# Decode attention: VectorE's eight unrolled heads become one loop whose semaphores are counted down

## The chip, the cores and the metric

One core of a Trainium2 chip. The metric is device time in microseconds (us) of one execution. A run is called fast when nothing marks it as slowed.

## The reference

```
B, Hq, Hkv, Sq, Sk, D = 1, 32, 8, 1, 65536, 128        # bf16 q, k, v
k = repeat(k, 4, axis=1); v = repeat(v, 4, axis=1)      # 4 query heads share one k/v head
scores = einsum("bhqd,bhkd->bhqk", q, k) * D ** -0.5
p = softmax(scores, axis=-1)
return einsum("bhqk,bhkd->bhqd", p, v)
```

k and v together are 268 MB and each byte is used once. Per k/v head there is one softmax over 65,536 keys for four query rows.

## The kernel before

`io` holds three slots of 64 KB per partition: slot 0 for half a head of v, slots 1 and 2 for the two halves (b = 0, 1) of a head of k. SyncE issues all loads on one DMA queue, in this order; each waits until PE has read what the slot held:

```
    load_k(0, 0); load_k(0, 1)
    for g in range(1, G):
        for b in range(2):
            load_k(g, b)          # waits for PE's scores of k(g-1, b):      s_sc
            load_v(g - 1, b)      # waits for PE's use of the v half before: s_vc
    load_v(G - 1, 0); load_v(G - 1, 1)
```

```
    def load_v(g, b):
        done = 2 * (2 * g + b)
        if (g, b) == (G - 1, 1):
            SP.wait((s_vc, done - 1))                     # first half of the last v
            load(v, g, b, 0, s_v[0], CUTS[0], CUTS[1])
            SP.wait((s_vc, done))
            ...                                           # the rest, in small pieces
        elif (g, b) in ((G - 2, 1), (G - 1, 0)):
            for i in range(2):                            # in two halves
                SP.wait((s_vc, done - 1 + i))
                load(v, g, b, 0, s_v[i], 128 * i, 128 * i + 128)
        else:
            SP.wait((s_vc, done))
            load(v, g, b, 0, s_v[0])
```

VectorE transposes k in place, finds the maximum, makes the bias, transposes the weights for PE (`weights`) and adds up the four partial sums of the output (`collect`). ACT does the exp and zeroes the PSUM accumulator (`clear`). PE already runs a loop. VectorE's program is unrolled by Python over the heads:

```
    for g in range(G):
        for _ in transposes(g, 0): pass
        for i, _ in enumerate(transposes(g, 1)):
            if i == 0 and g:
                DV.wait((s_vc, 4 * g - 2))
                weights(g - 1, 1)
        top(g)
        softmax(g)                       # issues ACT's exp too; for g == 0 also clear(0)
        if 0 < g < G - 1:
            weights(g, 0)
            DV.wait((s_vc, 4 * g))
            collected[g - 1] = collect()
            ACTQ.wait((s_dv, collected[g - 1]))
            clear(g)
        elif g:                          # the last head
            DV.wait((s_vc, 4 * g))
            DV.after(collect())
            collected[g - 1] = DV.mark(dve.memset(vacc, 0.0))
            weights(g, 0)
        else:                            # head 0: no collect
            weights(g, 0)
        if g: n_kept = keep(g - 1)
```

## Time and profile before

| | before |
|---|---|
| median of the first 3 runs | 630.67 us (630.35 to 631.05) |
| span of the profiled run | 628.4 us |
| bytes read | 268.44 MB, 427 GB/s over the span |
| VectorE busy | 54% |
| VectorE's program | 177 instructions |

From the page of the kernel before: the span, the DMA row (busy tenths in 40 slices of the span) and the list of DMA queues (kind: packets, MB, share of 16 engines).

```profile
span 628.4 us, 7102 instructions
...
DMA  8999999999999999999999999999999999999996
...
q1 hardware_dynamic: 6656, 268.45, 99.1%
q8 instruction: 1, 0.02, 0.0%
...
q14 instruction: 1, 0.01, 0.0%
```

The 16 DMA engines hardly ever rest (the packets of q1 fill 99.1% of their span), so the DMA queue is the bound here and everything else matters only if it leaves that queue, or one engine of it, without work. The page marks two packets as instruction; in the packet records they are 16,384 bytes at 624.0 us (queue 8) and 8,192 bytes at 221.2 us (queue 14). That such a packet is a part of a program being fetched is my reading; best_fetch below tests it for queue 14.

From the timeline of the kernel before (start us, duration us, engine, line, operation, tensors, count, and in brackets the idle time before it and what ended it): the end of head 0 with the v load that follows from it, a steady head, and the last head.

```profile
62.94 0.16 DVE L243 COPY nmb<-pb 128x1 f32<-128x1 f32 x1 [0.37 <-PE pb L462]
63.14 1.97 ACT L245 ACTIVATE ex<-acc,nmb 128x2048 bf16<-128x2048 f32 x1 [60.50 <-DVE nmb L243]
65.23 1.25 DVE L267 STREAM_TRANSPOSE et<-ex 128x1024 bf16<-128x1024 bf16 x1 [2.13 <-ACT ex L245]
65.29 2.31 ACT L256 ACTIVATE acc<-wz 128x2560 f32<-128x2560 bf16 x1
66.40 8.73 DVE L226 STREAM_TRANSPOSE io<-io 128x4096 uint32<-128x4096 uint32 x2
...
95.05 0.33 SPq L132 DMA_DIRECT2D io<-in_v_dram  x1
95.49 0.37 SPq L132 DMA_DIRECT2D io<-in_k_dram  x1
101.06 4.45 DVE L226 STREAM_TRANSPOSE io<-io 128x4096 uint32<-128x4096 uint32 x1 [17.29 <-DMA io<-in_k_dram]
...
372.73 17.30 DVE L226 STREAM_TRANSPOSE io<-io 128x8192 uint32<-128x8192 uint32 x2 [3.67 <-DMA io<-in_k_dram]
382.11 10.01 PE L420 MATMUL acc<-io,wz 128*128 x32 [9.65 <-PEq L114]
...
590.75 1.05 DVE L273 TENSOR_TENSOR vy<-acc,sely 128x512 f32<-128x512 f32 x1
590.87 1.97 ACT L245 ACTIVATE ex<-acc,nmb 128x2048 bf16<-128x2048 f32 x1 [63.27 <-DVE nmb L243]
591.83 0.69 DVE L279 TENSOR_REDUCE vs<-vy 128x128 f32<-128x512 f32 x1
592.70 0.48 DVE L313 MEMSET acc<- 128x512 f32 x1 [0.18 <-DVE vs L279]
593.37 0.59 PE L372 MATMUL pf<-vs,sel 128*4 128x130 f32 x2 [2.74 <-PEq L114]
595.66 3.59 PE L378 MATMUL acc<-io,et 128*16 128x512 bf16 x32 [1.70 <-PEq L114]
...
599.29 0.33 SPq L132 DMA_DIRECT2D io<-in_v_dram  x1
```

The second v of head 0 is issued at 95.05 us, and the k load ahead of it in the queue is seen by VectorE at 101.06: 6.0 us in hand. In a steady head VectorE waits 3.67 us for k. In the last head the first half of the last v is issued at 599.29 us.

### The profile page before, as it was taken

The numbers are of one execution on the slowest core, as the hardware profiler recorded it, in microseconds if no ns is written. First come the engines' busy times: TensorE is split into PE (matmuls) and PEld (weight loads), VectorE is DVE, ScalarE is ACT, GpSimd is POOL, SyncE is SP. The second block draws the span as 40 slices with busy tenths as digits, with TensorE's granted clock in tenths as the row PEclk, the third lists the DMA queues.
The fourth block names the chain that finished last, engine by engine and source line by source line (L and its number), as shares of the span: only waits on it lengthen the run. The fifth ranks groups of instructions, "written<-read, shape, count | busy, mean of one in ns | idle before, by whom it ended". The sixth has DMA issues, their size and how long they took to land. (4 is left out here: it accounts for less than half of the span.)

```text
span 628.4 us, 7102 instructions
## 1 busy us (share of the span) xinstructions
PE 349.1 (56%) x2126; PEld 137.0 (22%) x2126; DVE 339.2 (54%) x132; ACT 36.1 (6%) x32; POOL 7.5 (1%) x40
## 2 busy tenths in 40 slices
PE   0776482834837257372674816748066571876345
PEld 0222130311313023130221302213022230332112
DVE  3984835649065490654907548085570846684210
ACT  0000200020000200002000020000200002000100
POOL 1000000000000000000000000000000000000000
PEclk9999596976969769696696966959579695899666
DMA  8999999999999999999999999999999999999996
GB/s 368 434 467 401 405 463 405 463 413 455 421 446 413 455 405 463 401 467 401 467 401 467 401 467 401 463 405 463 405 463 405 463 405 463 401 436 434 434 434 271
DMA packets 6714, 268.48 MB, mean 427 GB/s; under 512 B 824, under 2 KB 1080, under 8 KB 1464
## 3 DMA queue, kind: packets, MB, share of 16 engines
q1 hardware_dynamic: 6656, 268.45, 99.1%
q8 instruction: 1, 0.02, 0.0%
q10 hardware_dynamic: 56, 0.01, 0.0%
q14 instruction: 1, 0.01, 0.0%
HBM read 268.44 MB, written 0.01 MB: 427 GB/s over the span
## 5 line engine op out<-in xcount | busy, mean ns | idle before, releaser
L420 PE MATMUL acc<-io,wz 128*128 x1024 | 269.2, 414 | 183.8 <-PEq L114 180.1
L226 DVE STREAM_TRANSPOSE io<-io 128x4096 uint32<-128x4096 uint32 (+1 forms) x54 | 279.0, 5207 | 164.9 <-DMA io<-in_k_dram 164.9
L420 PEld LDWEIGHTS acc<-io,wz 128*128 x1024 | 105.4, 103 | 347.8 <-issue 268.0
L378 PE MATMUL acc<-io,et 128*16 128x512 bf16 x1016 | 69.0, 416 | 22.1 <-PEq L114 21.5
L231 DVE TENSOR_REDUCE mg<-acc 128x1 f32<-128x2048 f32 x8 | 18.3, 2292 | 52.8 <-PE acc L420 52.8
L245 ACT ACTIVATE ex<-acc,nmb 128x2048 bf16<-128x2048 f32 x8 | 15.7, 1967 | 531.5 <-DVE nmb L243 531.5
L372 PE MATMUL pf<-vs,sel 128*4 128x130 f32 (+1 forms) x20 | 5.7, 386 | 62.6 <-PEq L114 62.6
L378 PEld LDWEIGHTS acc<-io,et 128*16 128x16 bf16 x1016 | 26.3, 94 | 61.4 <-issue 38.2
L267 DVE STREAM_TRANSPOSE et<-ex 128x1024 bf16<-128x1024 bf16 x16 | 19.6, 1224 | 29.7 <-ACT ex L245 14.9
L256 ACT ACTIVATE acc<-wz 128x2560 f32<-128x2560 bf16 x7 | 16.1, 2307 | 17.9 <-DVE vs L279 17.8
L372 PEld LDWEIGHTS pf<-vs,sel 128*4 128x4 f32 x20 | 1.2, 83 | 63.0 <-issue 63.0
L273 DVE TENSOR_TENSOR vy<-acc,sely 128x512 f32<-128x512 f32 x8 | 7.8, 980 | 11.9 <-PE acc L378 11.9
L235 DVE TENSOR_REDUCE m<-pt 1x4 f32<-1x128 f32 x8 | 2.2, 279 | 21.1 <-PE pt L460 21.1
L358 POOL COPY wz<-qT 32x16 bf16<-32x16 bf16 x32 | 6.1, 191 | 518.0 <-PE acc L420 435.5
L445 PE MATMUL pt<-et 128*16 128x512 bf16 x16 | 6.6, 410 | 0.0
L279 DVE TENSOR_REDUCE vs<-vy 128x128 f32<-128x512 f32 x7 | 4.8, 686 | 0.2
L462 PE MATMUL pb<-ident,nrow 1*128 1x1 f32 x8 | 1.5, 189 | 5.7 <-PEq L114 5.7
L460 PE MATMUL pt<-ident,mg 128*1 128x128 f32 x8 | 2.2, 270 | 2.5 <-PEq L114 2.5
L189 DVE MEMSET acc<- 128x2560 f32 x1 | 2.2, 2192 | 1.6 <-SPq L62 1.6
L243 DVE COPY nmb<-pb 128x1 f32<-128x1 f32 x8 | 1.3, 158 | 3.0 <-PE pb L462 3.0
L462 PEld LDWEIGHTS pb<-ident,nrow 1*128 1x128 f32 x8 | 1.1, 133 | 7.0 <-issue 7.0
L292 ACT ACTIVATE fall<-pf 4x130 f32<-4x130 f32 x7 | 1.9, 269 | 7.7 <-PE pf L372 7.7
(28 smaller groups left out, 17.8 us busy)
## 6 DMA issues: line engine op xcount, KB each, us to landing
io<-in_v_dram SPq DMA_DIRECT2D x5, 4096.0 KB, 16.8
io<-in_k_dram SPq DMA_DIRECT2D x4, 4096.0 KB, 25.9
io<-in_k_dram SPq DMA_DIRECT2D x4, 2048.0 KB, 40.3
io<-in_v_dram SPq DMA_DIRECT2D x1, 2048.0 KB, 10.8
io<-in_v_dram SPq DMA_DIRECT2D x1, 1024.0 KB, 12.9
io<-in_v_dram SPq DMA_DIRECT2D x3, 256.0 KB, 13.3
io<-in_v_dram SPq DMA_DIRECT2D x2, 128.0 KB, 13.3
io<-in_k_dram SPq DMA_DIRECT2D x13, 44.2
```

The source lines that it names most:

```text
L226: dve.transpose(out=part, in_=part).then_inc(s_kt, n // 32)
L231: dve.tensor_reduce(out=mg[:, :], in_=sc, axis=AX.X, op=ALU.max).then_inc(s_mg, 1)
L245: n = ACTQ.mark(act.activation(out=ex[:, :, :].rearrange("p b n -> p (b n)"), in_=sc, func=ACT.Exp, bias=nmb[:, :], scale=SCALE, accum_out ...
L256: cleared[g] = ACTQ.mark(act.activation(out=acc[:, :], in_=wz[:, 0, 0:1].to_broadcast([P, 5 * 512]), func=ACT.Copy))
L267: dve.transpose(out=et[:, :, :].rearrange("p i n -> p (i n)"), in_=ex[:, 2 * b:2 * b + 2, :].rearrange("p i n -> p (i n)"),).then_inc(s_et, 1)
L273: n = DV.mark(dve.tensor_tensor(out=vy[:, :, :].rearrange("p d y -> p y d") if not last else vz, in0=vacc, in1=sely[:, :, None].to_broadca ...
L279: return DV.mark(dve.tensor_reduce(out=vs[:, 0:D], in_=vy[:, :, :], axis=AX.X, op=ALU.add))
L358: gp.tensor_copy(out=wz[r, :, c0:c0 + H].rearrange("p (s w) h -> p s w h", s=2), in_=qTb[r, :, :, g, :],).then_inc(s_w, 1)
L372: return pe.matmul(out=pf[0:H, 0:w], lhsT=sel[:, :], rhs=vs[:, 0:w], skip_group_check=True, **kw)
L378: return pe.matmul(out=vacc[32 * c:32 * c + 16, :, :], lhsT=et[:, ch // 2, w0:w0 + 16], rhs=io[:, PS * ch + 4 * tt:PS * ch + 4 * tt + 4, : ...
L420: i = pe.matmul(out=bass.AP(acc, r_o, [[2560, P], [1, 512]]), lhsT=bass.AP(wz, r_w + ((2 * s + e) * WB - 4 * u), [[4 * WB, P], [1, P]]), r ...
L445: pe.matmul(out=pt[0:16, :], lhsT=et[:, 0, 0:16], rhs=et[:, 0, :], start=True, stop=True)
```

## The change

VectorE's program becomes one loop over the heads, 75 instructions in all, for 177. The loop's code has the same numbers to wait for in every pass, so each semaphore is taken down again after its wait, by an instruction of its own (the trace of the changed kernel has 116 EVENT_SEMAPHORE records on VectorE, the kernel before 25). What VectorE waits for must then be signalled once per head to VectorE alone: SyncE passes on "v half used" (`s_vd`), GpSimd "scores done" (`s_sd`).

```
-    for g in range(G):
-        ...                                    # the unrolled heads, as above
+    with nc.body("dve_head", valid_engines=only_d):
+        nc.regs_alu(r_g, r_g, 1, op=ALU.add)
+        transposes(0, 0, SL)                   # always pieces of 64, four per half
+        transposes(1, 0, 128)
+        d_take(s_vd)
+        weights(1)                             # in head 0 too, on zeros
+        transposes(1, 128, SL)
+        d_take(s_sd)
+        ...                                    # maximum, bias: d_take before each step
+        d_take(s_ex)
+        weights(0)
+        d_take(s_vd)
+        dve.tensor_tensor(out=vy..., in0=vacc, in1=sely..., op=ALU.mult).then_inc(s_ds, 1)
+        d_take(s_ds)
+        dve.tensor_reduce(out=vs[:, 0:D], in_=vy..., op=ALU.add).then_inc(s_dv, 1)
+        nc.br_cmp(r_g, G, "dve_head", "dve_tail", "IS_LT", engines=only_d)

+    for g in range(G):                         # ACT stays unrolled
+        ACTQ.wait((s_dv, d_nmb(g)))
+        act.activation(out=ex..., in_=sc, func=ACT.Exp, ...).then_inc(s_ex, 1)
+        ...
+        ACTQ.wait((s_dv, collected(g - 1)))
+        n_clear[g] = ACTQ.mark(act.activation(out=acc[:, :], in_=wz..., func=ACT.Copy))

     def load_v(g, b):
-            SP.wait((s_vc, done))
+            values_done(done)                  # the same wait, then sem_inc(s_vd, 1)
```

(Cut: the semaphores' counts given ahead, GpSimd's relay, a GpSimd memset of `ex`, PE's semaphore names.) Three things besides the loop move with it, since every pass must be alike: head 0 gets a `weights(1)` and a collect, and its clear now follows the collect; in the last head collect comes after `weights(0)`, not under the exp; and an ACT clear of 2560 columns takes the place of VectorE's 0.48 us memset.

More of the change, by code (lines that the diff above doesn't have):

```diff
@@ L12 @@
 PE = mybir.EngineType.PE
+DVE = mybir.EngineType.DVE
+POOL = mybir.EngineType.Pool
 P = 128
@@ L109 @@
     s_sc, s_pe, s_vb, s_vc = sem("s_sc"), sem("s_pe"), sem("s_vb"), sem("s_vc")
+    s_sd, s_vd, s_pt, s_ex, s_ds = sem("s_sd"), sem("s_vd"), sem("s_pt"), sem("s_ex"), sem("s_ds")
     def down(eng, which, s, n, wait=False):
@@ L134, in load, with values_done @@
         ).then_inc(s, 16)
-    k_cuts = {(0, 0): [0, 128, 256], (0, 1): [0, 128, 256], (G - 1, 1): [0, 64, 128, 192, 256]}
-    s_k = {(b, lo): sem(f"s_k{b}_{lo}") for b, lo in ((0, 0), (0, 128), (1, 0), (1, 64), (1, 128), (1, 192))}
-    k_count = {}
-    k_ready = {}
+    k_lo = {0: [0, 128], 1: [0, 64, 128, 192]}
+    s_k = {(b, lo): sem(f"s_k{b}_{lo}") for b in k_lo for lo in k_lo[b]}
     def load_k(g, b):
         SP.wait((s_sc, 16 * g - 8 + 8 * b if g else 0))
-        cuts = k_cuts.get((g, b), [0, SL])
+        if g == 1:
+            sp.sem_inc(s_k[b, 128], 16 * (G - 1 - b))
+        cuts = [0, 128, SL] if g == 0 else [0, 64, 128, 192, SL] if (g, b) == (G - 1, 1) else [0, SL]
         for lo, hi in zip(cuts, cuts[1:]):
-            k_ready[g, b, lo] = key = s_k[b, lo], k_count.get((b, lo), 0) + 16
-            k_count[b, lo] = key[1]
-            load(k, g, b, 1 + b, key[0], lo, hi)
+            load(k, g, b, 1 + b, s_k[b, lo], lo, hi)
+    def values_done(n):
+        SP.wait((s_vc, n))
+        if n:
+            sp.sem_inc(s_vd, 1)
     def load_v(g, b):
@@ L158, in load_v @@
         elif (g, b) in ((G - 2, 1), (G - 1, 0)):
-            for i in range(2):
-                SP.wait((s_vc, done - 1 + i))
-                load(v, g, b, 0, s_v[i], 128 * i, 128 * i + 128)
+            SP.wait((s_vc, done - 1))
+            load(v, g, b, 0, s_v[0], 0, 128)
+            values_done(done)
+            load(v, g, b, 0, s_v[1], 128, SL)
         else:
-            SP.wait((s_vc, done))
+            values_done(done)
             load(v, g, b, 0, s_v[0])
-            sp.sem_inc(s_v[1], 16)
     load_k(0, 0)
     load_k(0, 1)
-    sp.sem_inc(s_v[2], 16)
     for g in range(1, G):
@@ L182 @@
     GP.mark(gp.memset(vs[:, :], 0.0))
+    GP.mark(gp.memset(ex[:, :, :], 0.0))
     n = GP.mark(gp.memset(ident[:, :], 0.0))
@@ L188 @@
     ))
-    n = DV.mark(dve.memset(acc[:, :], 0.0))
-    collected = {-2: n, -1: n}
+    gp.sem_inc(s_vd, 2)
+    for s, n in ((s_k[1, 64], 16 * (G - 1)), (s_k[1, 192], 16 * (G - 1)), (s_v[1], 16 * (2 * G - 3)), (s_v[2], 16)):
+        gp.sem_inc(s, n)
+    DV.mark(dve.memset(acc[:, :], 0.0))
     DV.wait((s_gp, p_ident))
@@ L208, with d_nmb, collected @@
         ))
+    def d_nmb(g):
+        return d_qT + 2 * g + 1
+    def collected(g):
+        return d_qT + 2 * g + 4
+    d_last = collected(G - 2) + 6
     qTb = qT[:, :, :].rearrange("p s n -> p (s n)").bitcast(bf16).rearrange(
@@ L213 @@
     )
-    def transposes(g, b):
-        for t0 in range(0, SL, 128):
-            if (g, b, t0) in k_ready:
-                DV.wait(k_ready[g, b, t0])
-            n = 128 if 1 < g < G - 1 and b == 0 else 64
-            for t in range(t0, t0 + 128, n):
-                if t > t0 and (g, b, t) in k_ready:
-                    DV.wait(k_ready[g, b, t])
-                part = io[:, (1 + b) * SL + t:(1 + b) * SL + t + n, :]
-                part = part.rearrange("p t d -> p (t d)").bitcast(u32)
-                dve.transpose(out=part, in_=part).then_inc(s_kt, n // 32)
-            yield
@@ L229, in top @@
-    def top(g):
-        DV.wait((s_sc, 16 * g + 16))
-        dve.tensor_reduce(out=mg[:, :], in_=sc, axis=AX.X, op=ALU.max).then_inc(s_mg, 1)
-    def softmax(g):
-        DV.wait((s_pe, 3 * g + 2))
-        n = DV.mark(dve.tensor_reduce(
-            out=m4[:, :], in_=pt[0:1, 0:P].rearrange("o (x h) -> o h x", h=H), axis=AX.X, op=ALU.max
-        ))
-        DV.after(n)
-        dve.tensor_scalar_mul(
-            out=nrow[:, :, :], in0=m4[:, None, :].to_broadcast([1, 32, H]), scalar1=-SCALE
-        ).then_inc(s_nr, 1)
-        DV.wait((s_pe, 3 * g + 3))
-        d_nmb = DV.mark(dve.tensor_copy(out=nmb[:, :], in_=pb[:, 0:1]))
-        ACTQ.wait((s_dv, d_nmb))
-        n = ACTQ.mark(act.activation(
-            out=ex[:, :, :].rearrange("p b n -> p (b n)"), in_=sc, func=ACT.Exp,
-            bias=nmb[:, :], scale=SCALE, accum_out=vs[:, D + g % 2:D + g % 2 + 1],
-        ))
-        exped[g] = n
-        if g == 0:
-            ACTQ.wait((s_gp, p_ident))
-            ACTQ.after(n)
-            clear(0)
@@ L255, in clear @@
-    def clear(g):
-        cleared[g] = ACTQ.mark(act.activation(
-            out=acc[:, :], in_=wz[:, 0, 0:1].to_broadcast([P, 5 * 512]), func=ACT.Copy
-        ))
-    exped = {}
-    cleared = {}
-    def weights(g, b):
-        if b == 0:
-            DV.wait((s_ac, exped[g]))
-        dve.transpose(
-            out=et[:, :, :].rearrange("p i n -> p (i n)"),
-            in_=ex[:, 2 * b:2 * b + 2, :].rearrange("p i n -> p (i n)"),
-        ).then_inc(s_et, 1)
-    def collect(last=False):
-        n = DV.mark(dve.tensor_tensor(
-            out=vy[:, :, :].rearrange("p d y -> p y d") if not last else vz, in0=vacc,
-            in1=sely[:, :, None].to_broadcast([P, 4, D]), op=ALU.mult,
-        ))
-        DV.after(n)
-        if not last:
-            return DV.mark(dve.tensor_reduce(
-                out=vs[:, 0:D], in_=vy[:, :, :], axis=AX.X, op=ALU.add
-            ))
-        n = DV.mark(dve.tensor_tensor(
-            out=vz[:, 0:2, :], in0=vz[:, 0:2, :], in1=vz[:, 2:4, :], op=ALU.add
-        ))
-        DV.after(n)
-        return DV.mark(dve.tensor_tensor(
-            out=vs[:, 0:D], in0=vz[:, 0, :], in1=vz[:, 1, :], op=ALU.add
-        ))
@@ L290, in keep @@
-    def keep(g):
-        ACTQ.wait((s_pe, 3 * g + 7))
-        return ACTQ.mark(act.activation(out=fall[:, g, :], in_=pf[0:H, 0:D + 2], func=ACT.Copy))
-    for g in range(G):
-        for _ in transposes(g, 0):
-            pass
-        for i, _ in enumerate(transposes(g, 1)):
-            if i == 0 and g:
-                DV.wait((s_vc, 4 * g - 2))
-                weights(g - 1, 1)
-        top(g)
-        softmax(g)
-        if 0 < g < G - 1:
-            weights(g, 0)
-            DV.wait((s_vc, 4 * g))
-            collected[g - 1] = collect()
-            ACTQ.wait((s_dv, collected[g - 1]))
-            clear(g)
-        elif g:
-            DV.wait((s_vc, 4 * g))
-            DV.after(collect())
-            collected[g - 1] = DV.mark(dve.memset(vacc, 0.0))
-            weights(g, 0)
-        else:
-            weights(g, 0)
-        if g:
-            n_kept = keep(g - 1)
@@ L319 @@
-    DV.wait((s_ac, n_kept), (s_vc, 4 * G - 2))
-    weights(G - 1, 1)
-    o7 = io[0:H, SL:SL + G - 1, :]
-    for i in range(2):
-        n = DV.mark(dve.reciprocal(out=r7[:, i::2], in_=fall[:, i::2, D + i]))
-    DV.after(n)
-    n = DV.mark(dve.tensor_tensor(
-        out=o7, in0=fall[:, :, 0:D], in1=r7[:, :, None].to_broadcast([H, G - 1, D]),
-        op=ALU.mult,
-    ))
-    SP.wait((s_dv, n))
-    sp.dma_start(
-        out=out[0, 0:(G - 1) * H, 0, :].rearrange("(g h) d -> h g d", h=H), in_=o7
-    ).then_inc(s_st, 16)
@@ L334 @@
-    DV.wait((s_vb, 2 * G))
-    collected[G - 1] = collect(True)
-    DV.wait((s_pe, 3 * G + 2))
-    d_rl = DV.mark(dve.reciprocal(out=rl[:, :], in_=pl))
-    ACTQ.wait((s_dv, d_rl), (s_pe, 3 * G + 3))
-    n = ACTQ.mark(act.activation(out=o[:, :], in_=fin, func=ACT.Copy, scale=rl[:, :]))
-    ACTQ.after(n)
-    act.dma_start(out=out[0, (G - 1) * H:G * H, 0, :], in_=o[:, :]).then_inc(s_st, 16)
-    ACTQ.wait((s_st, 32))
-    for g in range(G):
-        if g == 0:
-            GP.wait((s_dv, d_qT))
-            GP.after(p_ident)
-        else:
-            GP.wait((s_sc, 16 * g))
-        for a in range(4):
-            r = slice(32 * a, 32 * a + 32)
-            c0 = 28 + 32 * a
-            if a == 3:
-                GP.wait(
-                    (s_dv, collected[g - 2]), (s_ac, cleared.get(g - 1, 0))
-                )
-            gp.tensor_copy(
-                out=wz[r, :, c0:c0 + H].rearrange("p (s w) h -> p s w h", s=2),
-                in_=qTb[r, :, :, g, :],
-            ).then_inc(s_w, 1)
@@ L362, with take @@
-    GP.wait((s_sc, 16 * G), (s_dv, collected[G - 2]), (s_ac, exped[G - 1]))
-    gp.sem_inc(s_w, 4)
-    def take(s, n):
-        down(pe, PE, s, n, wait=True)
+    def take(eng, which, s, n=1):
+        down(eng, which, s, n, wait=True)
     IO = 3 * SL * D
@@ L398 @@
     with block("pe_head"):
-        take(s_w, 4)
+        take(pe, PE, s_w, 4)
         gather(D + 2, start=True, stop=True).then_inc(s_pe, 1)
@@ L415 @@
         r_o = o8 * 16
-        take(s_kt, 1)
+        take(pe, PE, s_kt, 1)
         for u in range(2):
@@ L433 @@
     with block("pe_values"):
-        take(s_et, 1)
+        take(pe, PE, s_et, 1)
         for ch in range(4):
@@ L438 @@
             elif ch != 1:
-                take(s_v[ch // 2], 16)
+                take(pe, PE, s_v[ch // 2], 16)
             for tt in range(16 if ch < 3 else (SL - TAIL) % PS // 4):
@@ L458 @@
     with block("pe_softmax"):
-        take(s_mg, 1)
-        pe.transpose(out=pt[0:1, 0:P], in_=mg[:, :], identity=ident[:, :]).then_inc(s_pe, 1)
-        take(s_nr, 1)
+        take(pe, PE, s_mg, 1)
+        pe.transpose(out=pt[0:1, 0:P], in_=mg[:, :], identity=ident[:, :]).then_inc(s_pt, 1)
+        take(pe, PE, s_nr, 1)
         pe.transpose(
             out=pb[:, 0:1], in_=nrow[:, :, :].rearrange("o x h -> o (x h)"), identity=ident[0:1, 0:1]
-        ).then_inc(s_pe, 1)
+        ).then_inc(s_pt, 1)
         nc.br("pe_head", engines=only)
@@ L468 @@
         out=pl, lhsT=sel[:, :], rhs=vs[:, D + (G - 1) % 2:D + (G - 1) % 2 + 1], start=True, stop=True
-    ).then_inc(s_pe, 1)
+    ).then_inc(s_pt, 1)
     for t in range(SL - TAIL, SL):
@@ L474 @@
         if t == CUTS[-2]:
-            pe.wait_ge(s_dv, collected[G - 1])
+            pe.wait_ge(s_dv, d_last)
             gather(D, start=False, stop=False)
@@ L482, with d_take, transposes, weights @@
     i.then_inc(s_pe, 1)
+    def d_take(s, n=1):
+        take(dve, DVE, s, n)
+    def transposes(b, lo, hi):
+        for t in range(lo, hi, 64):
+            if t in k_lo[b]:
+                d_take(s_k[b, t], 16)
+            part = io[:, (1 + b) * SL + t:(1 + b) * SL + t + 64, :].rearrange("p t d -> p (t d)").bitcast(u32)
+            dve.transpose(out=part, in_=part).then_inc(s_kt, 2)
+    def weights(b):
+        dve.transpose(
+            out=et[:, :, :].rearrange("p i n -> p (i n)"),
+            in_=ex[:, 2 * b:2 * b + 2, :].rearrange("p i n -> p (i n)"),
+        ).then_inc(s_et, 1)
@@ new lines @@
+    only_d = OrderedEngineSet([DVE])
+    r_g = nc.alloc_registers("g", engines=only_d)
+    nc.regs_mov(r_g, 0)
+    nc.br("dve_head", engines=only_d)
+    with nc.body("dve_head", valid_engines=only_d):
[6 more added lines that the diff above has]
+        d_take(s_sd)
+        dve.tensor_reduce(out=mg[:, :], in_=sc, axis=AX.X, op=ALU.max).then_inc(s_mg, 1)
+        d_take(s_pt)
+        dve.tensor_reduce(
+            out=m4[:, :], in_=pt[0:1, 0:P].rearrange("o (x h) -> o h x", h=H), axis=AX.X, op=ALU.max
+        ).then_inc(s_ds, 1)
+        d_take(s_ds)
+        dve.tensor_scalar_mul(
+            out=nrow[:, :, :], in0=m4[:, None, :].to_broadcast([1, 32, H]), scalar1=-SCALE
+        ).then_inc(s_nr, 1)
+        d_take(s_pt)
+        dve.tensor_copy(out=nmb[:, :], in_=pb[:, 0:1]).then_inc(s_dv, 1)
+        d_take(s_ex)
+        weights(0)
+        d_take(s_vd)
+        dve.tensor_tensor(
+            out=vy[:, :, :].rearrange("p d y -> p y d"), in0=vacc,
+            in1=sely[:, :, None].to_broadcast([P, 4, D]), op=ALU.mult,
+        ).then_inc(s_ds, 1)
+        d_take(s_ds)
+        dve.tensor_reduce(out=vs[:, 0:D], in_=vy[:, :, :], axis=AX.X, op=ALU.add).then_inc(s_dv, 1)
+        nc.br_cmp(r_g, G, "dve_head", "dve_tail", "IS_LT", engines=only_d)
@@ new lines @@
+    nc.switch_bb("dve_tail")
+    DV.n = collected(G - 2)
+    n_clear, n_kept = {}, 0
+    for g in range(G):
+        ACTQ.wait((s_dv, d_nmb(g)))
+        act.activation(
+            out=ex[:, :, :].rearrange("p b n -> p (b n)"), in_=sc, func=ACT.Exp,
+            bias=nmb[:, :], scale=SCALE, accum_out=vs[:, D + g % 2:D + g % 2 + 1],
+        ).then_inc(s_ex, 1)
+        if g == 0:
+            ACTQ.wait((s_gp, p_ident))
+        ACTQ.wait((s_dv, collected(g - 1)))
+        n_clear[g] = ACTQ.mark(act.activation(
+            out=acc[:, :], in_=wz[:, 0, 0:1].to_broadcast([P, 5 * 512]), func=ACT.Copy
+        ))
+        if g:
+            ACTQ.wait((s_pe, g + 2))
+            n_kept = ACTQ.mark(act.activation(
+                out=fall[:, g - 1, :], in_=pf[0:H, 0:D + 2], func=ACT.Copy
+            ))
@@ new lines @@
+    DV.wait((s_ac, n_kept), (s_vd, 1))
+    weights(1)
+    o7 = io[0:H, SL:SL + G - 1, :]
+    for i in range(2):
+        n = DV.mark(dve.reciprocal(out=r7[:, i::2], in_=fall[:, i::2, D + i]))
+    DV.after(n)
+    n = DV.mark(dve.tensor_tensor(
+        out=o7, in0=fall[:, :, 0:D], in1=r7[:, :, None].to_broadcast([H, G - 1, D]),
+        op=ALU.mult,
+    ))
+    SP.wait((s_dv, n))
+    sp.dma_start(
+        out=out[0, 0:(G - 1) * H, 0, :].rearrange("(g h) d -> h g d", h=H), in_=o7
+    ).then_inc(s_st, 16)
@@ new lines @@
+    DV.wait((s_vb, 2 * G))
+    n = DV.mark(dve.tensor_tensor(
+        out=vz, in0=vacc, in1=sely[:, :, None].to_broadcast([P, 4, D]), op=ALU.mult
+    ))
+    DV.after(n)
+    n = DV.mark(dve.tensor_tensor(
+        out=vz[:, 0:2, :], in0=vz[:, 0:2, :], in1=vz[:, 2:4, :], op=ALU.add
+    ))
+    DV.after(n)
+    n = DV.mark(dve.tensor_tensor(
+        out=vs[:, 0:D], in0=vz[:, 0, :], in1=vz[:, 1, :], op=ALU.add
+    ))
+    assert n == d_last
+    DV.wait((s_pt, 1))
+    d_rl = DV.mark(dve.reciprocal(out=rl[:, :], in_=pl))
@@ new lines @@
+    ACTQ.wait((s_dv, d_rl), (s_pe, G + 2))
+    n = ACTQ.mark(act.activation(out=o[:, :], in_=fin, func=ACT.Copy, scale=rl[:, :]))
+    ACTQ.after(n)
+    act.dma_start(out=out[0, (G - 1) * H:G * H, 0, :], in_=o[:, :]).then_inc(s_st, 16)
+    ACTQ.wait((s_st, 32))
+    for g in range(G):
+        if g == 0:
+            GP.wait((s_dv, d_qT))
+            GP.after(p_ident)
+        else:
+            GP.wait((s_sc, 16 * g))
+            gp.sem_inc(s_sd, 1)
+        for a in range(4):
+            r = slice(32 * a, 32 * a + 32)
+            c0 = 28 + 32 * a
+            if a == 3 and g == 1:
+                take(gp, POOL, s_et)
+            if a == 3 and g:
+                GP.wait((s_ac, n_clear[g - 1]))
+            gp.tensor_copy(
+                out=wz[r, :, c0:c0 + H].rearrange("p (s w) h -> p s w h", s=2),
+                in_=qTb[r, :, :, g, :],
+            ).then_inc(s_w, 1)
@@ L486 @@
+    GP.wait((s_sc, 16 * G))
+    gp.sem_inc(s_sd, 1)
+    GP.wait((s_ac, n_clear[G - 1]))
+    gp.sem_inc(s_w, 4)
 _INS = ['q', 'k', 'v']
```

## The prediction

> What bounds the kernel now. The DMA engines. The page shows them 90% busy or more in every slice but the first and the last, 268.45 MB in a span of 628.4 us. The chain of waits ends in the last loads of v (landing at 622.3 us) and about 3.5 us of PE and ACT. At a head's end VectorE still waits 3.66 us for the next k (timeline, 369.08 to 372.73), and a v load is issued 5.7 to 9.9 us before the loads queued ahead of it have landed. So small delays on VectorE are covered.
>
> What the change removes. [...]the page lists one instruction packet of 0.01 MB on queue 14, and the packet records place it about 221 us into the span. The 64 KB data packet beside it took 3.08 us, its neighbours 2.42 us. From then on one of the 16 DMA engines is 0.75 us behind, for good, since no engine idles: its last data packet ends 0.8 us after the next engine's. [...]this lag sits on the final chain. [...]I take the fetch to be VectorE's; it goes away. Worth 0.7 us.
>
> What it adds.
> - Countdown waits: instructions of their own, [...] Covered by the 3.66 us.
> - Transposes of k(b=0) in four pieces, not two (17.42 us against 17.30): PE starts some 4 us earlier in five heads; no gain, since DMA bounds.
> - Head 0: one more weights transpose (1.2 us) and collect (1.7 us), so the first matmuls of head 1 come 1.7 us later and the v load issued at 95.05 us moves to 96.8; the queue has work until 101. GpSimd's memset of ex (about 2 us) falls into the 7.75 us that VectorE waits for the first k. Covered.
> - The branch back: [...]no refetch.
> - Last head: before, collect overlapped the exp, and a 0.48 us VectorE memset cleared; the gather ran at 593.37 us. Now weights(0), collect, a 2.31 us ACT clear and a relay follow each other: gather at about 598.8, v matmuls (3.59 us) at 599.5 instead of 595.66. The first half of the last v is issued at about 603.1 instead of 599.28, while the half before it lands at about 604.6. An issue takes about 1.5 us to first data (start of the run), so the DMA may idle 0 to 0.5 us here, the one place where the longer chain can show; I charge 0.2 us.
>
> Sum: 630.67 - 0.7 + 0.2 = about 630.1 us; 629.4 to 630.9 in 8 of 10. Faster by over 2%: 0.01; within 2%: 0.98; slower by over 2%: 0.01.
>
> What would show it. The DMA list has no instruction packet on queue 14 within the span; no single DMA engine lags at the end; the v landing in the final chain comes some 0.5 us earlier; the last head's gather is near 598.8 us and the v issue after it near 603; each head's first k reaches PE about 4 us sooner.
>
> What would make it wrong: the branch back stalls VectorE by over 4 us per head, the v issue in the last head falls over 1.5 us behind, or the page fetched at 221 us is not VectorE's.

What the trace of the kernel before shows: the packet on queue 14 has 8,192 bytes and begins at 221.2 us; in the loads' landing times, the last of 16 is 0.22 us behind the median at 197.7 us and 0.96 us at 237.2; and PE's wait for v on `s_v[2]`, in the final chain, ends at 622.38 us, after the last of the 16 landings of that load (622.34) and not after the median one (621.37). That the packet is VectorE's and worth 0.7 us was an estimate from that lag, 0.75 us in the packet records. The memset of `ex`, "about 2 us", took 1.81 us in the changed kernel's trace.

## The result

Six runs of each: 631.77 us median (630.22 to 632.80) against 630.65 (630.28 to 631.36). The ratio is 1.0017, 95% interval 1.0002 to 1.0031: within 2% as forecast, but outside the range, and on the other side of the kernel before. A ratio here is the mean time of one kernel's fast runs over that of the other's of the same rounds, so it isn't quite the ratio of the medians.

The page of the changed kernel, the same rows:

```profile
span 630.3 us, 7233 instructions
...
DMA  8999999999999999999999999999999999999986
...
q1 hardware_dynamic: 6656, 268.45, 98.8%
q8 instruction: 1, 0.02, 0.0%
```

The packet on queue 14 is gone, as predicted. But the DMA row has an 8 in its second last slice, where the kernel before has a 9: something ran dry near the end.

The timeline of the changed kernel, the same places:

```profile
63.56 0.16 DVE L394 COPY nmb<-pb 128x1 f32<-128x1 f32 x1 [0.49 <-DVEq L118]
65.96 1.25 DVE L366 STREAM_TRANSPOSE et<-ex 128x1024 bf16<-128x1024 bf16 x1 [2.24 <-DVEq L118]
67.13 1.02 DVE L399 TENSOR_TENSOR vy<-acc,sely 128x512 f32<-128x512 f32 x1
68.29 0.69 DVE L404 TENSOR_REDUCE vs<-vy 128x128 f32<-128x512 f32 x1
68.90 8.76 DVE L363 STREAM_TRANSPOSE io<-io 128x4096 uint32<-128x4096 uint32 x2
69.08 2.31 ACT L421 ACTIVATE acc<-wz 128x2560 f32<-128x2560 bf16 x1 [3.26 <-DVE vs L404]
...
97.65 0.33 SPq L136 DMA_DIRECT2D io<-in_v_dram  x1
98.03 0.42 SPq L136 DMA_DIRECT2D io<-in_k_dram  x1
100.37 4.45 DVE L363 STREAM_TRANSPOSE io<-io 128x4096 uint32<-128x4096 uint32 x1 [14.06 <-DVEq L118]
...
372.94 17.43 DVE L363 STREAM_TRANSPOSE io<-io 128x4096 uint32<-128x4096 uint32 x4 [3.10 <-DVEq L118]
378.06 7.34 PE L290 MATMUL acc<-io,wz 128*128 x24 [4.88 <-PEq L118]
...
593.64 1.25 DVE L366 STREAM_TRANSPOSE et<-ex 128x1024 bf16<-128x1024 bf16 x1 [2.24 <-DVEq L118]
594.81 1.01 DVE L399 TENSOR_TENSOR vy<-acc,sely 128x512 f32<-128x512 f32 x1
595.97 0.69 DVE L404 TENSOR_REDUCE vs<-vy 128x128 f32<-128x512 f32 x1
596.69 2.31 ACT L421 ACTIVATE acc<-wz 128x2560 f32<-128x2560 bf16 x1 [3.20 <-DVE vs L404]
599.19 0.59 PE L242 MATMUL pf<-vs,sel 128*4 128x130 f32 x2 [8.10 <-PEq L118]
600.03 3.59 PE L248 MATMUL acc<-io,et 128*16 128x512 bf16 x32 [0.26 <-PEq L118]
...
603.66 0.33 SPq L136 DMA_DIRECT2D io<-in_v_dram  x1
```

Three readings. The steady head is as forecast: VectorE still waits 3.10 us for k, and PE starts 4 us sooner (378.06 for 382.11). In head 0 the transposes start 2.50 us later (68.90 for 66.40): 0.73 us of it was there when `weights(0)` began (65.96 for 65.23), from the slower waits (in the rows, 0.49 for 0.37 us and 2.24 for 2.13) and a 0.28 us later start of the head's end; the rest is the collect. So the v load comes at 97.65 us, 2.6 us later, with 2.7 us in hand and not 6.0. In the last head that v half comes at 603.66 us, 4.4 us later.

**What one DMA engine did.** The busy rows average 16 engines. The trace also has every data packet with start, duration and size, without its engine; but the data packets fill 99.1% of the 16 engines' span (98.8% in the changed kernel), so they can be strung together, each to the chain that had just ended. That gives 16 chains and, where a chain pauses, an idle time. The lists below are worked out that way; their clock starts about 11 us before the span. Before, one chain pauses for 0.31 us for the instruction packet, then has a slow packet (3.08 us for 64 KB, its neighbours 2.42). In the changed kernel:

```
one chain    idle 1.11 us at 110.7, its next packet 3.23 us (others 2.42)     second v of head 0
15 chains    idle 0.8 to 2.9 us at 614 to 617, then 1.5 to 2.0 us for 32 KB (others 1.21)   last v
```

The load of 97.65 us finds one of 16 engines already idle. The chain with that pause is 1.72 us behind the median chain when the last head begins, has no pause over 0.3 us in the dry stretch, and still ends last of all: 1.0 us after the median chain. It isn't untouched there, though: its own landings come 1.4 us late after the dry stretch (see "What the landings show").

### The profile page after: what moved, and what is told of

Read it like the earlier page. It is cut to its first block, busy times and chain, and to the rows that moved or that the text cites. A ratio compares the mean times of both kernels' runs of the same rounds, so it can differ in the third digit from the quotient of the medians.

```text
span 630.3 us, 7233 instructions
## 1 busy us (share of the span) xinstructions
PE 344.1 (55%) x2126; PEld 135.7 (22%) x2126; DVE 342.2 (54%) x144; ACT 38.5 (6%) x33; POOL 9.3 (1%) x41
## 3 DMA queue, kind: packets, MB, share of 16 engines
q1 hardware_dynamic: 6656, 268.45, 98.8%
## 5 line engine op out<-in xcount | busy, mean ns | idle before, releaser
L363 DVE STREAM_TRANSPOSE io<-io 128x4096 uint32<-128x4096 uint32 x64 | 279.6, 4415 | 157.0 <-DVEq L118 157.0
L248 PE MATMUL acc<-io,et 128*16 128x512 bf16 x1016 | 66.1, 403 | 20.2 <-PEq L118 18.9
L421 ACT ACTIVATE acc<-wz 128x2560 f32<-128x2560 bf16 x8 | 18.5, 2307 | 25.6 <-DVE vs L404 25.6
```

Source lines behind the costliest of these rows:

```text
L248: return pe.matmul(out=vacc[32 * c:32 * c + 16, :, :], lhsT=et[:, ch // 2, w0:w0 + 16], rhs=io[:, PS * ch + 4 * tt:PS * ch + 4 * tt + 4, : ...
L363: dve.transpose(out=part, in_=part).then_inc(s_kt, 2)
L421: n_clear[g] = ACTQ.mark(act.activation(out=acc[:, :], in_=wz[:, 0, 0:1].to_broadcast([P, 5 * 512]), func=ACT.Copy))
```

## The experiments

First theory: the late issue in the last head costs the time. Rival: the loop itself does, a little in every head (counting waits, relays, branch back). Twelve kernels ran; the kernel before ran beside, with medians 630.70, 630.27 and 630.69 us.

For each trace the table gives when the second v of head 0 was issued, when VectorE saw the k load ahead of it, how many chains then idled over 0.3 us, how far the last chain was behind the median chain about 595 us, the idle time of the chains in the last head (median, longest), and when the last chain ended, counted from the first data packet. Times are medians of all the label's runs; the rest is read from one traced run per label. Where chains nearly touch they can be confused, so the lags of split01 and before_head0 are taken from the times at which the engines reported a load as landed.

| kernel | v issued | k seen | chains idle there | furthest behind | last head idle | last chain's end | time |
|---|---|---|---|---|---|---|---|
| before | 95.05 | 101.06 | 0 | 0.94 (fetch) | 0, 0.1 | 622.67 | 630.65 |
| changed | 97.65 | 100.37 | 1 | 1.72 | 1.7, 2.9 | 624.11 | 631.77 |
| both | 95.90 | 101.06 | 0 | 0.81 | 0, 0 | 621.93 | 630.77 |
| short_clear | 97.66 | 100.38 | 3 | 1.87 | 0, 0.3 | 623.09 | 632.19 |
| two_more_clears | 97.70 | 100.84 | 2 | 2.05 | 6.7, 7.1 | 628.96 | 636.61 |
| before_late | 95.11 | 100.32 | 0 | 1.12 (fetch) | 0.4, 1.4 | 622.06 | 630.07 |
| split01 | 95.89 | 101.56 | 0 | 1.25 | 1.2, 2.0 | 623.28 | 631.31 |
| split01_short | 95.60 | 100.34 | 0 | 0.18 | 0, 0 | 621.26 | 629.99 |
| head0_more | 99.25 | 100.44 | 16 | 0.35 | 0, 0.9 | 623.51 | 631.54 |
| before_head0 | 97.51 | 100.27 | 1 | 1.96 | 0, 0.1 | 623.27 | 632.26 |
| best | 93.94 | 101.09 | 0 | 0.82 | 0, 0 | 622.25 | 631.03 |
| best_fetch | 93.86 | 100.99 | 0 | 0.17 | 0, 0 | 622.65 | 631.33 |
| best_straddle | 94.10 | 101.50 | 0 | 0.69 | 0, 0 | 622.82 | 630.89 |
| after_again | 97.68 | 100.39 | 3 | 1.69 | 1.6, 2.1 | 623.65 | 632.45 |

### Is it the last head?

**both**: the loop stays; the collect moves under the exp, and the last clear is cut.

```
-        d_take(s_ex); weights(0)
         d_take(s_vd); ...collect...
+        d_take(s_ex); weights(0)
...
-        act.activation(... Exp ...).then_inc(s_ex, 1)
+        n = ACTQ.mark(act.activation(... Exp ...)); ACTQ.after(n); act.sem_inc(s_ex, 1)
...
-            out=acc[:, :], in_=wz[:, 0, 0:1].to_broadcast([P, 5 * 512])
+            out=acc[:, c0:], ...                 # c0 = 2048 in the last head, else 0
```

> The changed kernel with its two last-head delays taken away: collect runs before weights(0), under the exp, in every head, and the last head's ACT clear writes the 512 columns of the output sums, not 2560. My theory (the DMA engines run dry in the last head because the first half of the last v is issued too late): last gather near 595 us instead of 599.2, that v issue near 599.5 instead of 603.7, no idle stretch of the DMA engines near the end, no instruction packet: about 629.9 us, 0.7 below the kernel before. Rival (the loop itself costs: countdown waits, relays and the branch back, a little in every head): it keeps them all, so about 631.8 us as in the changed kernel.

Measured: 630.77 us (630.29 to 631.14), ratio to before 1.0000 (0.9986 to 1.0013). Keeping the loop and losing the delays takes the slowdown away, so a cost of the loop in every head, the rival, falls; the hoped-for 0.7 us below before didn't come. The edit also moves the load of head 0 back to 95.90 us, so it doesn't tell the two places apart. A first build of this edit had no wait of ACT on its own exp; the check found the race and it didn't run.

**short_clear**: only the last head's ACT clear, cut from 2.31 to 0.60 us as above.

> Only the last head's ACT clear is cut to 512 columns, from 2.31 us to about 0.6 us. Theory: the v issue comes 1.7 us earlier, near 602.0 us, and most of the dry stretch (1.9 us as a mean over the engines) goes: about 630.4 us. Rival (loop costs): no change, 631.8 us.

Measured: 632.19 us (631.16 to 632.61), ratio 1.0018 (1.0004 to 1.0031). The timeline of this kernel has the v half 1.83 us earlier than the changed kernel's 603.66:

```profile
601.83 0.33 SPq L136 DMA_DIRECT2D io<-in_v_dram  x1
```

The dry stretch is gone (one chain over 0.3 us) and the time didn't fall. What remains is in the table: three chains idled at the second v of head 0, and the furthest is 1.87 us behind. I concluded that the first theory, that the last head makes the time, is wrong. The trace doesn't bear that out: the last data landed at 625.45 us, 1.1 us sooner than in the changed kernel (626.53). The gain was lost after the landing, in PE's last 28 matmuls; first the changed kernel, then this one:

```profile
624.59 2.17 PE L348 MATMUL pf<-io,et 128*4 128x128 bf16 x28
...
623.58 3.15 PE L348 MATMUL pf<-io,et 128*4 128x128 bf16 x28
```

PE's granted clock is 1.0 of full speed there in the changed kernel and 0.5 in this one (623.2 to 626.7 us). Only one run of each kernel was traced, so it isn't known whether the other runs of short_clear had the slow clock too.

**two_more_clears**: two more 2.31 us clears in the last head of the changed kernel, each after the one before.

> The changed kernel with two more 2.31 us ACT clears after the one of the last head (harmless, they write the same zeros). Theory: the gather and the v issue come about 4.8 us later and the DMA engines idle that much longer: about 636.5 us. Rival (loop costs): ACT is not on its path, 631.8 us.

Measured: 636.61 us (635.78 to 638.99), ratio 1.0098 (1.0074 to 1.0122). The load came 5.6 us later than in the changed kernel (609.26 us), and the last data landed 5.0 us later (631.56): nearly the whole delay reaches the end, so the lag of one engine was hiding little of it.

**before_late**: the unrolled kernel with the changed kernel's last head.

```
-        if 0 < g < G - 1:
+        if g:                                    # weights(0), collect, ACT clear
...
-        elif g:
-            ...collect, VectorE memset, weights(g, 0)
```

> The kernel before, fully unrolled VectorE, with the changed kernel's order in the last head alone: weights(0), then collect, then an ACT clear of 2560 columns in place of the 0.48 us VectorE memset. Theory: gather near 598.7 us, v issue near 603, DMA engines dry for about 1.5 us: about 631.8 us, the slowdown without any loop. Rival (loop costs): no loop, so 630.7 us.

Measured: 630.07 us (629.77 to 631.39), ratio 0.9997 (0.9983 to 1.0011): a clear miss of my forecast. The load came at 602.30 us, 3 us later than before, and most chains did idle (0.4 us in the median, 1.4 at most). But the chain delayed by the instruction fetch was 1.12 us behind and had no pause; when the others were idle it caught up. The dry stretch was paid by engines that had time in hand. The theory that replaces the first: **the end sees the chain that is furthest behind; delays on different engines don't add up, the largest counts.** And in the changed kernel, I then thought, the largest comes from head 0. The landings below show that in its traces the last head came last.

### Is it head 0?

**split01**: the changed kernel, with the second v of head 0 loaded in two halves, the first issued as soon as PE has used the upper half of the slot.

```
-        elif (g, b) in ((G - 2, 1), (G - 1, 0)):
+        elif (g, b) in ((0, 1), (G - 2, 1), (G - 1, 0)):
```

(and the counts of `s_v[1]` that SyncE and GpSimd give to fit; a build that gave them all at the start had a race.)

> The changed kernel, but v of head 0, second half, is loaded in two halves, the first issued once the upper half of its buffer is read, near 95.6 us instead of 97.65. The short clear gained nothing, so the new theory: what the end sees is the one DMA engine that is furthest behind, and in the changed kernel one to three engines fall 1.5 to 2 us behind where that v load starts, since it is issued 2.4 us before the queue has run out[...]. The late issue in the last head is then second. New theory: no engine falls behind near 100 us, the dry stretch of the last head stays and decides: 631.1 us, 0.7 below the changed kernel. Old theory (the last head alone): 631.8 us.

Measured: 631.31 us (630.59 to 631.79), ratio 1.0010 (0.9998 to 1.0023), between before and changed. In its trace no chain idles at that load. It has a chain 1.3 us behind for another reason, from about 42 us on, where the first k of head 1 starts; see below.

**split01_short**: that and the short last clear, loop as in the changed kernel.

> The two halves and the last head's short clear together; the loop is that of the changed kernel. New theory: both causes are gone and no fetch is left: 629.9 to 630.6 us, as fast as the kernel before or up to 0.8 us faster. Rival (loop costs in every head): 631.8 us.

Measured: 629.99 us (629.53 to 630.88), ratio 0.9996 (0.9984 to 1.0009). From its timeline, the two issues:

```profile
95.60 0.33 SPq L136 DMA_DIRECT2D io<-in_v_dram  x1
...
600.10 0.33 SPq L136 DMA_DIRECT2D io<-in_v_dram  x1
```

With both loads in time no chain is more than 0.18 us behind at 595 us, and the last chain's end, 621.26 us after the first data, is the earliest of all traces. The same loop, at the pace of the kernel before. (Its last data landed 1.3 us sooner than the kernel before's, 623.66 for 624.99; 0.6 us of that is lost again at the program's end, see below.)

**before_head0**: the opposite: the unrolled kernel, with a collect put into head 0 ahead of its clear.

```
         else:
             weights(g, 0)
+            DV.after(collect())
+            collected[g - 1] = DV.mark(dve.tensor_reduce(...))    # the reduction once more
+            ACTQ.wait((s_dv, collected[g - 1]))
+            clear(g)                                             # moved here from softmax(0)
```

> The kernel before, unrolled, with a collect in head 0 ahead of its clear as in the changed kernel (its final reduction done twice, to make up for the slower waits of the loop), so that the v load issued at 95.05 us comes near 97.6 us. The last head is left as it was. New theory: one to three engines fall 1.5 to 2 us behind near 100 us and the end moves with them: about 631.6 us. Old theory (last head alone) and the loop rival: 630.7 us.

Measured: 632.26 us (631.18 to 632.75), ratio 1.0025 (1.0012 to 1.0037): as slow as the changed kernel, without the loop and with the last head untouched. Its timeline:

```profile
97.51 0.33 SPq L132 DMA_DIRECT2D io<-in_v_dram  x1
```

One chain idles 1.36 us there; another loses 1.1 us about 177 us for no reason that I found. The furthest is 2.4 us behind at first and 1.96 at 595 us, and ends 1.9 us after the median chain. But in this trace the last data landed only 0.7 us later than in the kernel before (625.67 for 624.99). Another 0.9 us went after it, where PE's granted clock was 0.5 again. So the late load alone makes the data late; that it makes the whole slowdown isn't shown.

**head0_more**: the changed kernel with a second ACT clear in head 0.

> The changed kernel with a second 2.31 us ACT clear in head 0 alone. New theory: the v load issued at 97.65 us moves to about 100 us, when the queue is just empty, so all engines idle some 1.5 to 2 us and some up to 4: 633 to 634 us. Old theory (last head alone): nothing that is done in head 0 reaches the end, 631.8 us.

Measured: 631.54 us (631.18 to 633.10), ratio 1.0015 (1.0000 to 1.0029). A miss: delaying the load further cost nothing more. The timeline:

```profile
99.25 0.33 SPq L136 DMA_DIRECT2D io<-in_v_dram  x1
```

The trace shows why. Now all 16 chains idle, 0.4 to 1.8 us, and start again within about 0.9 us of each other: nobody is far behind (0.35 us). And only two chains idle over 0.3 us in the last head, although PE's v matmuls there start as late as in the changed kernel (599.86 against 600.03). PE's last-head work waits for landings, and so for the slowest engine (in the kernel before, its wait on `s_v[2]` ends at 622.38 us, after the last of the 16 landings at 622.34); I read it so that with one engine 1.7 us behind, the other 15 run out of packets that much too early for the next issue. Three other traces have the same late last head and a chain 1.3 to 1.7 us behind (changed, after_again, split01): their median idle there is 1.2 to 1.7 us, against 0.02 us here. No run varied that alone. The late last head cost here too: from the landing near 605 us to the last one took 20.64 us, 0.9 us more than in the traces without it.

### The fetch, the loop's place, and a repeat

**best**: the mends of both and of split01.

> All three mends on the changed kernel: collect under the exp in every head, the last head's clear cut to 512 columns, the second v of head 0 in two halves. Theory (the end sees the DMA engine that is furthest behind; late issues put engines behind): v issue of head 0 near 94 us, no engine behind, no dry stretch: 629.5 to 630.3 us. Rival (loop costs in every head): at least as slow as the changed kernel less what the last head gave, 631 us or more.

Measured: 631.03 us (630.70 to 631.20), ratio 1.0006 (0.9993 to 1.0020). No chain idles at the two loads, but a chain is 0.8 us behind, again from about 42 us on. So the version with all mends isn't shown to beat the kernel before, nor is split01_short: their intervals include 1.

**best_fetch**: best with 72 one-element memsets between loop and tail, which makes VectorE's program 75 + 72 = 147 instructions.

> The same with 72 one-element memsets after the loop, where VectorE waits some 11 us[...]. If the fetch of the kernel before was VectorE's second page, one instruction packet appears again within the span, and one DMA engine is 0.75 us behind from there on: 0.3 to 0.7 us above the run with the three mends. If the fetch belonged to another engine: no packet, no difference.

Measured: 631.33 us (630.71 to 631.71), ratio 1.0011 (0.9998 to 1.0025); against best +0.30 us in the median, intervals overlapping. The DMA list of this kernel:

```profile
q8 instruction: 1, 0.02, 0.0%
...
q14 instruction: 1, 0.01, 0.0%
```

In the packet records an 8,192-byte packet lies at about 598 us, just after the loop; one chain idles 0.31 us and needs 1.88 us for its next 32 KB (others 1.21), and ends 0.86 us after the next one. Before that no chain was far behind (0.17 us). In best, split01 and split01_short an instruction packet of queue 14 is listed too, but its record lies at the very end, behind the data. So the fetch in mid-run does come with a longer program of VectorE (147 instructions here; with the 75 of best no packet is in mid-run; no run shows where between them the limit lies), and it costs one engine about 0.9 us (0.86 in this trace). How much of that reaches the time is smaller than these runs resolve.

**best_straddle**: that and 16 memsets ahead of the loop, 163 instructions.

> The same again with 16 more memsets ahead of the loop[...]. If every branch back across the boundary of a fetched block costs a fetch, an instruction packet appears in every head, each putting one engine up to 0.75 us behind and stalling VectorE: 632 us or more. If the loop stays resident wherever it lies, one packet at most: as the run with 72 memsets after the loop, within 0.5 us.

Measured: 630.89 us (630.40 to 631.87), ratio 1.0006 (0.9991 to 1.0021). One packet in mid-run, at about 598 us, none in the loop: the branch back fetched nothing. Whether the loop lay across a boundary of fetched blocks in this run isn't shown.

**after_again**: the changed kernel, unedited.

> The changed kernel once more, unedited, for a second trace and a time on the same chip as the three mends. Theory: again one to three engines fall 1.5 us or more behind where the second v of head 0 starts, and the end is set by them: 631.8 us. If that trace shows no engine behind there and the time is still 631.8 us, the theory is wrong.

Measured: 632.45 us (631.10 to 633.10), ratio 1.0028 (1.0014 to 1.0041). Three chains idled 0.9 to 1.3 us at the second v of head 0; the furthest was 1.69 us behind.

**What the landings show.** The trace keeps 16 landing times for each load (in the kernel before, 256 for the 16 loads on `s_v[0]`). I read each as one engine's share: in each of its loads that landed between 236 and 620 us, the last of the 16 lies 0.95 to 0.96 us behind the median. So the furthest engine can be read without stringing packets. All times are us of the span, from one traced run each: when the first half of the last v was issued; when the furthest engine landed the load ahead of it; when the last data of all landed; from there to the end of PE's last matmul; and from that to the end of the span.

| kernel | last head's issue | furthest lands, near 605 | last landing | PE after it | end after PE |
|---|---|---|---|---|---|
| before | 599.29 | 605.24 | 624.99 | 0.69 | 2.67 |
| before_late | 602.30 | 604.59 | 624.46 | 0.81 | 2.66 |
| before_head0 | 599.58 | 605.95 | 625.67 | 1.60 | 2.67 |
| changed | 603.66 | 605.35 | 626.53 | 0.67 | 3.09 |
| after_again | 603.83 | 605.47 | 626.07 | 0.92 | 3.09 |
| short_clear | 601.83 | 605.74 | 625.45 | 1.75 | 3.08 |
| split01 | 603.51 | 605.15 | 625.70 | 0.86 | 3.32 |
| split01_short | 600.10 | 603.78 | 623.66 | 0.65 | 3.31 |

Three readings, which change the account above:

- **The later of two limits sets the last landing.** In nine of the 14 traces it comes 19.7 to 19.9 us after the furthest engine's landing near 605 us: there the engine furthest behind decides. In the other five (changed, after_again, split01, head0_more, two_more_clears) the last head's load was issued at 603.38 us or later, and the last landing comes 22.2 to 22.9 us after that issue, with the furthest engine anywhere from 0.3 to 2.0 us behind. So in both traces of the changed kernel the last head decided. With the furthest engine alone the last data would have landed 1.4 and 0.8 us sooner. Mending one place leaves the other: 625.45 (short_clear) or 625.70 (split01), and 623.66 with both mended.
- **The looped program ends more slowly.** From PE's end to the end of the span it needs 0.4 us more, and 0.65 with the split load. Most of the 0.4 us lies between the first two semaphore instructions of GpSimd in the closing barrier, 0.44 us apart for 0.08. No run varied this; the cause is open.
- **PE's clock at the end differs between traces.** PE needs 1.6 to 1.75 us after the last landing in short_clear, before_head0 and head0_more, where its granted clock was 0.5, and at most 1.0 us in the other eleven.

The changed kernel's traced span is 1.94 us longer than the kernel before's: 1.54 to the last landing, none in PE, 0.42 at the end. In after_again it is 1.72: 1.08, 0.23 and 0.42. These are single traces; the two unrolled ones without a late head 0 differ by 0.5 us in the last landing.

## Why the prediction was wrong

- **DMA bounds, steady heads have slack, relays and counted waits are covered there: right.** VectorE still waits 3.10 us per head (3.67 before), and split01_short keeps every counted wait, relay and branch at 629.99 us.
- **PE starts 4 us sooner, no gain: right** (378.06 against 382.11 us).
- **The fetch is VectorE's and goes away: right.** Its packet is in mid-run in all three unrolled traces (at about 221, 221 and 184 us), in none of the nine looped ones of 75 instructions, and again in best_fetch and best_straddle, of 147 and 163. Its worth of 0.7 us wasn't seen: it is one engine's delay, which counts only while nothing else is later (before_late had both it, 1.12 us, and a last load 3 us later, at 630.07 us), and in the changed kernel head 0 and the last head both were. In split01_short, where neither is left, the last data did land 1.3 us sooner than in the kernel before, in one trace each.
- **The step that failed:** "the v load issued at 95.05 us moves to 96.8; the queue has work until 101 ... Covered." It moved to 97.65: 2.6 us, not 1.7, since I left the slower waits out of head 0's sum, and they had put `weights(0)` 0.73 us back (with the 0.28 us later start). The queue's work was seen done at 100.37. And 2.7 us in hand isn't covered. The only lead I knew was the 1.5 us from issue to first data of an idle machine at the start of the run (in the packet records 1.0 us for the first engine and 1.8 for the last); with the engines busy, 1 to 3 of 16 had no work in time (they idled 0.4 to 1.6 us), in all four traces of that order with the issue at 97.65 to 97.70 us (changed, after_again, short_clear, two_more_clears) and in before_head0. With the slow packet that followed (3.23 us for 2.42 in the changed kernel), the furthest was 1.5 to 2.4 us behind the median chain after it, and still 1.7 to 2.0 us behind 475 us later. Mending this issue and the last clear restores the time (split01_short), the late issue alone makes the last data 0.7 us late in the unrolled kernel (before_head0); mending it alone in the changed kernel gave 1.0010 with an interval that holds both 1 and most of the loss (split01).
- **The last head, charged 0.2 us: the mechanism right, the size wrong, and the second step that failed.** Gather at 599.19 (forecast 598.8), issue at 603.66 (603.1), dry 1.7 us in the median (0 to 0.5). In the two traces of the changed kernel this set the last landing, 1.4 and 0.8 us after what the furthest engine alone would have given. Yet it isn't paid as a term of a sum: mended alone it leaves the engine that head 0 put behind (short_clear), and with the issue at 602.30 us in the unrolled kernel it cost next to nothing, since the engine delayed by the fetch was as late (before_late).
- **Missing from the sum:** the end of the program, 0.4 us longer in the traces of the changed kernel.

Put as sums: I added -0.7 and +0.2. The two aren't added; the later of the limits counts. A fetch delay of about 0.9 us was exchanged for one of about 1.7 us from head 0 and for a last load 4.4 us later, which came later still; the program's end added 0.4 us. The time moved by about 1.1 us in the median.

Open: what puts one or two chains 0.6 to 1.3 us behind at about 42 us in both, two_more_clears, split01, best and best_straddle (5 of 11 looped traces, 0 of 3 unrolled). It is the start of another load, the first k of head 1; no run varied that issue. It may be part of why best isn't faster; another part is its program's end, 0.66 us longer than before's. The slower end itself is open, and so is whether PE's slow clock at the end, seen in three traces, belongs to these kernels or to these runs. Also open is how much lead is enough: 2.7 us wasn't, 4.7 us and more was for this load.

## What to carry to other kernels

In a kernel bound by loads over many queues or engines, ask of each load how long before the queue's end it is issued, and in the first and last pass too, where the order differs from the steady ones. A uniform loop body moves work into those passes; that, more than the loop itself, was what cost here (split01_short keeps the loop at 629.99 us). And with all engines busy (99.1% of the span here), a small delay of one engine stayed (in the kernel before 0.96 us from 237 us to 620, 0.87 in the last load), while two such delays didn't add (before_late, 630.07 us): look for the engine that is furthest behind, and for the load that is issued last, before adding or subtracting microseconds. A time that doesn't fall doesn't yet refute a cause: look in the trace where the gain went.
